# Masks added to the scores by TensorE for half of the batches, and all sixteen early weight tiles decoded in PSUM

## The chip, the cores and the metric

One Trainium2 chip; the kernel uses one of its cores. The metric is device time in microseconds (us) for one execution, and shorter is better. The engines are TensorE (PE in the profile, its weight loads PEld), VectorE (DVE), ScalarE (ACT), GpSimd (POOL) and the queue that issues most transfers (SP). SBUF is the on-chip memory; PSUM, eight banks of 128 partitions by 2 KB, is where TensorE writes.

## The reference

Three stages on 2304 tokens (4 batches of 576):

```python
def _attn_ref(q, k, v):                 # B, H, S, D = 4, 8, 576, 64
    ...
    q_d = q.reshape(B, H, Sd, factor, D).mean(axis=3)     # factor 4, Sd 144
    ...
    out_up = np.repeat(sm_attn(q_d, k_d, v_d), factor, axis=2)
    mask = np.abs(pos[:, None] - pos[None, :]) < factor
    scores = np.where(mask, scale * np.matmul(q, k.transpose(0, 1, 3, 2)), -1000000000.0)
    scores = scores - np.max(scores, axis=-1, keepdims=True)
    attn = np.exp(scores)
    attn = attn / (np.sum(attn, axis=-1, keepdims=True) + 1e-09)
    return out_up + np.matmul(attn, v)
# first feed-forward:  h = x @ w_in;  y = (h * sigmoid(h)) @ w_out     512 -> 2048 -> 512
# second feed-forward: h = x @ w_in2; y = elu(h) @ w_out2              512 -> 2048 -> 512
```

## The kernel before, in words

**Attention.** Sixteen pairs of heads, four per batch, each a call of `attend` (line 563). For one pair: rows of q and k are loaded, transposed by TensorE (line 635) and copied to SBUF; ten windows of 64 by 64 local scores per head go to two PSUM banks, one per head (line 747); VectorE multiplies each bank by a scale, adds the mask and writes the sum to SBUF (`add_mask`, line 758, twice), takes row maxima (line 766, 640 columns for both heads), GpSimd subtracts them (`across`, line 771), ScalarE takes exp (line 777), VectorE sums and inverts (lines 781 to 783), GpSimd multiplies (line 771 again), TensorE transposes (line 853) and multiplies by v (line 920). A pooled branch of 144 by 144 scores runs beside it: sums of q and k on VectorE (line 677), scores (line 800), maxima (line 814), exp (line 822), inverse (lines 832, 833), a scaling on GpSimd (line 839), transposes (line 874), product with pooled v (line 892). Pooled v of batches 1 to 3 comes from two GpSimd additions (lines 709, 710) or from one VectorE reduction (line 714), whichever engine the planner finds free. Both branches are joined into x by VectorE (line 930).

**Weights.** All products of the feed-forward layers are made of three fp32r products of high and low parts, so each weight tile must be split. Before that, the first layer's sixteen tiles of 128 by 1024 words pass a decoder (`decode_jobs`, line 393, called by `prepare`, line 1040): ScalarE takes an absolute value into a temporary (line 411) and converts the low words (line 415), then three steps that need each other: `second`, a clamp (line 419), `third` (line 422) and `fourth` (line 426), both on VectorE. The high part is then copied by ScalarE (line 1054) and the low part subtracted by GpSimd or VectorE (line 1058).

```python
temp = Hold(banks, "w") if i < N_PSUM else None              # prepare, N_PSUM = 8
b = Job("V", 0.70 if inner else 0.45, second, [a], other=None if inner or i >= 2 * FP else ("G", 1.1, lambda: second(nc.gpsimd)))
```

For tiles 0 to 7 the temporary is a PSUM bank (in the rows: `b<-b`), and the clamp is VectorE's; for tiles 8 to 15 it is the SBUF tile `wf`, and the clamp may go to GpSimd.

**Feed-forward during attention.** Six blocks of 256 tokens by eight groups of 256 hidden columns give 48 units (`unit`, line 1068): 12 products into a bank (line 1077), tanh (line 1105), the SiLU product (line 1106) on VectorE, split into high and low (lines 1108, 1111), 12 products into two bank-long accumulators of the block (line 1125). Blocks 0 and 1 run interleaved and need the sixteen tiles one by one. After the last unit, ten passes of 768-column pairs follow (lines 1453, 1541, 1543), which take the rest of the time.

**Who sets the order.** Nothing is ordered by the chip: a planner in the kernel keeps jobs with an engine, a duration, predecessors, PSUM banks they take and use, and due times, and emits them one by one, each to its engine's queue (`pick`, line 293). At any time at most two banks may hold decoder temporaries and at most three unit sums (`bank_rule`, line 344). `LATE` shifts the due times of units of the first two blocks between their two halves. Until unit (0, 0) is emitted, the planner puts products of a zero tile into gaps that it foresees on TensorE (`filler`, line 352); they write to the bank that has been free longest.

Of the kernel before, what the change touches and what calls it, by code (L numbers as in the profile page):

```python
# [22 lines left out]
def attention_moe_moe2_kernel(ctx, tc, q, k, v, wi1, wo1, wi2, wo2, out):  # L23
# [76 lines left out]
    ident = att.tile([P, P], F32, name="ident")  # L100
    mask = att.tile([P, NW // 2, WIN], F32, name="mask")
    xa = xpool.tile([P, KC, 2 * S], F32, tag="xa", name="xa")
# [19 lines left out]
    def constants():  # L122
        make_identity(nc, ident)
        tmp = t_tiles[1][:, :4 * WIN].rearrange("p (n w) -> p n w", w=WIN)
        nc.gpsimd.memset(tmp, 0.0)
        for n, (half, low, high) in enumerate([(0, 0, 6), (0, -3, 3), (1, 0, 6), (1, -3, 3)]):

            for sign, bound in ((1, -low), (-1, high)):
                nc.gpsimd.affine_select(
                    out=tmp[:, n, :], in_=tmp[:, n, :], compare_op=ALU.is_ge, fill=MASKED,  # L130
                    base=bound + sign * WIN * half, pattern=[[sign, WIN]], channel_multiplier=-sign,
                )
        for s in range(NW // 2):
# [218 lines left out]
    def filler(n):  # L352
        if n > 0:
            entry = min(banks.free, key=lambda x: x[:2])
            for _ in range(n):
                nc.tensor.matmul(entry[2], wz[0][:, :P], wz[0][:, :512], start=True, stop=True)

    def fill(t):
        gap = t - clock_of["P"]
        if banks.free:  # L360
            filler(min(int((gap - 0.1) / 0.22), 40))

    wz = []


# [27 lines left out]
    def decode_jobs(i, out, preds, takes=(), temp=None):  # L393
# [169 lines left out]
    def attend(i, due):  # L563
# [171 lines left out]
        for part, (s0, s1, halves_, outs) in enumerate(parts):  # L735
# [18 lines left out]
            psl = follow(Job("P", 0.15 + 0.11 * (s1 - s0) * 2, scores, copies, lat=0.2, takes=held + ([hE] if start_ else []), uses=[hqk], mode="s"), "psl")  # L754
            masked = []
            for j, bank in enumerate(held):
                def add_mask(j=j, bank=bank, s0=s0, s1=s1):
                    nc.vector.scalar_tensor_tensor(
                        E4(s0, s1)[:, :, j, :], bank.tile[:, :(s1 - s0) * WIN].rearrange("p (s w) -> p s w", w=WIN), BSCALE,
                        mask[:, s0:s1], op0=ALU.mult, op1=ALU.add,  # L760
                    )

                masked.append(Job("V", 0.15 + 0.00106 * (s1 - s0) * WIN, add_mask, [psl], uses=[bank]))
            n = 2 * (s1 - s0) * WIN
            top = Job(
                "V", 0.14 + 0.00106 * n, lambda s0=s0, s1=s1: nc.vector.tensor_reduce(col3(hmx, s0, s1), E3(s0, s1), axis=AX.X, op=ALU.max),
                masked, takes=[hmx] if start_ else [], uses=[hmx],
            )
# [4 lines left out]
            less = alike(  # L773
                0.15 + 0.00173 * n, lambda f=across: f(nc.gpsimd, hmx, ALU.subtract),
                0.15 + 0.00106 * n, lambda f=across: f(nc.vector, hmx, ALU.subtract), [top], main="G", uses=[hmx],
            )
            ex = Job("A", 0.21 + 0.00083 * n, lambda s0=s0, s1=s1: nc.scalar.activation(E3(s0, s1), E3(s0, s1), AF.Exp), [less])

# [786 lines left out]
    with tc.manual_schedule():  # L1565
# [138 lines left out]
```

## Time and profile before

| | us |
|---|---|
| median of 3 runs (892.75 to 894.23) | 893.6 |
| the profiled execution, its own time | 893.9 |
| its span (first to last instruction) | 891.5 |
| PE busy in the span | 875.7 (98%) |
| DVE, ACT, POOL busy in the span | 673.1, 540.8, 273.0 |

A row of the profile names line, engine, operation, and the tiles as output <- inputs without their buffer numbers. "Busy" is the union of an engine's instructions; matmuls overlap each other, so a busy PE may still run below its pace. What lies around the span is 2.4 us (893.9 less 891.5).

### The profile page before, as it was taken

Reading aid. Unit: us, or ns where it says so; the run is one execution under the profiler, and the core shown is the slowest. Engines: PE = TensorE matmul, PEld = TensorE weight load, DVE = VectorE, ACT = ScalarE, POOL = GpSimd, SP = SyncE. Lnnn points to the kernel's source line nnn. Section 1 sums busy time; section 2 is a strip of 40 time slices with the busy share of each in tenths; the row PEclk is TensorE's granted clock in tenths of the full one; section 3 lists DMA queues with packets and bytes.
Section 4 is the critical chain, followed back from the end, with each engine's and each line's share of the span. In section 5 each row is a group of like instructions: output and inputs, shape, how many; then the busy total and the mean of one; then the engine's idle time right before and its main releaser. Section 6 shows DMA issues by size and latency. Waiting matters only on the chain.

```text
span 891.5 us, 17228 instructions
## 1 busy us (share of the span) xinstructions
PE 875.7 (98%) x6614; PEld 817.0 (92%) x6614; DVE 673.1 (76%) x1236; ACT 540.8 (61%) x1226; POOL 273.0 (31%) x278
## 2 busy tenths in 40 slices
PE   9989899999999999999999999999999999999998
PEld 6778798999999999999999999898898998998986
DVE  6899768786967988968848969489489888483562
ACT  4796546664547668648347477286497584571650
POOL 4687977875301211401014213001051031010000
PEclk9999899999999999999999999999999999999999
DMA  9896148551134345154432240350520430220301
GB/s 158 217 220 159 54 107 240 119 143 36 69 95 142 106 142 177 48 201 154 130 112 90 83 155 23 107 178 3 186 71 37 165 131 36 90 89 35 107 1 72
DMA packets 105522, 100.08 MB, mean 112 GB/s; under 512 B 62240, under 2 KB 92448, under 8 KB 105312
## 3 DMA queue, kind: packets, MB, share of 16 engines
q1 hardware_dynamic: 103072, 98.39, 37.2%
q8 instruction: 52, 0.85, 0.4%
q10 hardware_dynamic: 2368, 0.59, 0.4%
q14 instruction: 30, 0.25, 0.1%
HBM read 75.37 MB, written 23.59 MB: 111 GB/s over the span
## 4 chain that ended last, share of the span: by engine, by line
PE 90%; DVE 4%; POOL 2%; ACT 1%; DMA 1%; issue 1%; SPq 0%; POOLq 0%; DVEq 0%; ACTq 0%
PE b L1453 33%; PE b L1543 22%; PE b L1541 15%; PE b L1125 6%; PE b L1077 6%; PE b L635 1%; PE b L892 1%; PE b L920 1%; PE b L874 1%; PE b L800 1%; POOL w L1058 1%; PE b L853 1%; PE b L747 1%; DMA nat<-in_q_dram 1%; POOL wf L419 1%
## 5 line engine op out<-in xcount | busy, mean ns | idle before, releaser
L1543 PE MATMUL b<-w,grw 128*128 128x512 f32 x384 | 121.2, 389 | 0.0
L1543 PE MATMUL b<-w,ghk 128*128 128x512 f32 x288 | 99.1, 389 | 0.0
L1453 PE MATMUL b<-xhr,xaw 128*128 128x384 f32 x360 | 96.4, 335 | 0.0
L1541 PE MATMUL b<-grw,w 128*128 128x384 f32 x352 | 91.2, 334 | 0.0
L1543 PEld LDWEIGHTS b<-w,grw 128*128 128x128 f32 x384 | 72.1, 188 | 14.9
L1077 PE MATMUL b<-xh,w 128*128 128x256 f32 x384 | 84.5, 298 | 0.8 <-DVE t L1106 0.8
L1453 PE MATMUL b<-xhr,w 128*128 128x384 f32 x320 | 83.8, 335 | 0.0
L1125 PE MATMUL b<-gh,w 128*128 128x256 f32 x384 | 80.7, 292 | 0.0
L1543 PE MATMUL b<-w,glk 128*128 128x512 f32 x192 | 74.8, 389 | 0.0
L1541 PE MATMUL b<-ghk,w 128*128 128x384 f32 x248 | 71.6, 334 | 0.0
L1077 PEld LDWEIGHTS b<-xh,w 128*128 128x128 f32 x384 | 66.1, 198 | 2.2 <-DVE t L1106 1.2
L1235 POOL TENSOR_TENSOR w<-raw,w 128x512 fp32r<-128x512 f32 x16 | 22.8, 1435 | 144.9 <-ACT w L1233 129.8
L1453 PE MATMUL b<-xlr,xaw 128*128 128x384 f32 x200 | 66.9, 334 | 0.0
L1125 PEld LDWEIGHTS b<-gh,w 128*128 128x128 f32 x384 | 64.1, 193 | 1.5 <-issue 1.2
L1453 PEld LDWEIGHTS b<-xhr,xaw 128*128 128x128 f32 x360 | 65.4, 188 | 0.0
L1543 PEld LDWEIGHTS b<-w,ghk 128*128 128x128 f32 x288 | 54.1, 188 | 11.2
L1541 PEld LDWEIGHTS b<-grw,w 128*128 128x128 f32 x352 | 63.7, 188 | 0.0
L1465 ACT COPY hg<-b 128x384 f32<-128x384 f32 x60 | 28.5, 479 | 50.2 <-PE b L1453 49.2
L1453 PEld LDWEIGHTS b<-xhr,w 128*128 128x128 f32 x320 | 58.0, 188 | 0.2
L1236 DVE TENSOR_TENSOR xlr<-tail,xhr 128x768 fp32r<-128x768 f32 x51 | 49.6, 972 | 11.4 <-ACT xhr L1233 10.8
L1506 DVE SCALAR_TENSOR_TENSOR part<-b,part 128x384 f32<-128x384 f32 (+1 forms) x42 | 25.0, 608 | 43.2 <-PE b L1543 28.4
L1541 PE MATMUL b<-glk,w 128*128 128x384 f32 x168 | 56.1, 334 | 0.0
(262 smaller groups left out, 2443.2 us busy)
## 6 DMA issues: line engine op xcount, KB each, us to landing
ws<-in_moe_w_in_dram SPq DMA_DIRECT2D x32, 512.0 KB
ws<-in_moe_w_out_dram SPq DMA_DIRECT2D x31, 512.0 KB
tail<-x SPq DMA_DIRECT2D x24, 384.0 KB
x<-part SPq DMA_DIRECT2D x6, 768.0 KB
out_dram<-part SPq DMA_DIRECT2D x18, 256.0 KB
vw<-in_v_dram SPq DMA_DIRECT2D x28, 144.0 KB
tail<-xd SPq DMA_DIRECT2D x10, 384.0 KB
natv<-in_v_dram SPq DMA_DIRECT2D x22, 144.0 KB
```

The source lines that it names most:

```text
L419: eng.tensor_scalar(tf, tf, 2.0, W_MAX, op0=ALU.max, op1=ALU.min)
L635: nc.tensor.transpose(bank.tile[:, n * TB:(n + 1) * TB], row(which, c)[:TB], ident[:TB, :TB])
L747: nc.tensor.matmul(held[j].tile[o:o + WIN, c:c + WIN], qT[j * D:(j + 1) * D, q0[w]:q0[w] + WIN], kT[j * D:(j + 1) * D, w0[w]:w0[w] + WIN], ...
L1077: nc.tensor.matmul(ph.tile[:, :NB0], w[a][:, c, :], x_slot(n, c, b_), start=start and m == 0, stop=stop and m == len(products) - 1,)
L1125: nc.tensor.matmul(y[d // 2].tile[:, o:o + NB0], w[m // 2][:, sl], gg(m % 2), start=f == 0 and m == 0 and d % 2 == 0, stop=fin and m == 2, ...
L1235: "G", GPS_[width], lambda: nc.gpsimd.tensor_tensor(lo(), src, hi().bitcast(F32), ALU.subtract), [a], due=due,
L1236: other=("V", VEC_[width], lambda: nc.vector.tensor_tensor(lo(), src, hi().bitcast(F32), ALU.subtract)),
L1453: nc.tensor.matmul(acc_, a[:, cs], b[:, c, :], start=fresh and c == 0 and m == 0, stop=c == 1 and m == 2, skip_group_check=True,)
L1465: snap[after, j] = [Job("A", ACT_[NB], lambda dst=dst, acc_=acc_: nc.scalar.copy(dst, acc_), [], gate, due=soon)]
L1506: nc.vector.scalar_tensor_tensor(dst, src, sc, dst, op0=ALU.mult, op1=ALU.add)
L1541: nc.tensor.matmul(y[d][:, :NB], wm[:, sl], gm, start=first, stop=last_)
L1543: nc.tensor.matmul(y[d], gm[:, sl], wm, start=first, stop=last_)
```

## The change

1. For batches 0 and 1 (`MASK_PE = 2`) TensorE puts the mask into both score banks before the scores: four products per pair of heads, each of a 64 by 64 unit matrix with 320 columns of a bf16 mask; the scores are accumulated on top. VectorE then takes the maxima straight from each bank (two reductions of 128x320) and subtracts them from each bank (two instructions of 128x320); the scale moves into the exp. The GpSimd subtraction of these eight pairs is gone. Four VectorE instructions at the start build the second half of the mask and the unit matrix.
2. All sixteen weight tiles use a PSUM bank as the decoder's temporary (`N_PSUM = 16`), and the clamp is always VectorE's.
3. The products of zeros write to one bank of their own, which is held until unit (0, 0) is emitted.
4. `LATE` is 1.2 instead of 1.0.

```diff
-    QUAD_FROM = 2
+    QUAD_FROM, MASK_PE = 2, 2
...
-    LATE, FRAC = 1.0, (0.25, 0.5, 0.75, 1.0)
-    SLACK, MOST_H, N_PSUM, SPLIT_F = 0.05, 3, 8, 3
+    LATE, FRAC = 1.2, (0.25, 0.5, 0.75, 1.0)
+    SLACK, MOST_H, N_PSUM, SPLIT_F = 0.05, 3, 16, 3
...
+        for p in range(0, P, WIN):
+            nc.vector.tensor_copy(masks[p:p + WIN, 1], mask[WIN - p:P - p])
+            nc.vector.tensor_copy(unit_[p:p + WIN, :], ident[p:p + WIN, p:p + WIN])
...
     def filler(n):
         if n > 0:
-            entry = min(banks.free, key=lambda x: x[:2])
             for _ in range(n):
-                nc.tensor.matmul(entry[2], wz[0][:, :P], wz[0][:, :512], start=True, stop=True)
+                nc.tensor.matmul(fill_bank.tile, wz[0][:, :P], wz[0][:, :512], start=True, stop=True)
...
-        b = Job("V", 0.70 if inner else 0.45, second, [a], other=None if inner or i >= 2 * FP else ("G", 1.1, lambda: second(nc.gpsimd)))
+        b = Job("V", 0.70 if inner else 0.45, second, [a])
...
+                if b < MASK_PE:
+                    for j in range(2):
+                        for o in range(2):
+                            nc.tensor.matmul(
+                                held[j].tile[o * WIN:(o + 1) * WIN, :(s1 - s0) * WIN], unit_[j * WIN:(j + 1) * WIN, :],
+                                masks[j * WIN:(j + 1) * WIN, o ^ j, s0:s1].rearrange("p s w -> p (s w)"),
+                                start=True, stop=False, skip_group_check=True,
+                            )
...
-                            start=True, stop=True,
+                            start=b >= MASK_PE, stop=True, skip_group_check=b < MASK_PE,
...
+            if b < MASK_PE:
+                for j in range(2):
+                    top = Job(
+                        "V", 0.14 + 0.00053 * n, lambda j=j, mx4=mx4, bank3=bank3: nc.vector.tensor_reduce(mx4(j), bank3(j), axis=AX.X, op=ALU.max),
...
+                    def minus(j=j, mx4=mx4, bank3=bank3, s0=s0, s1=s1):
+                        nc.vector.tensor_tensor(E4(s0, s1)[:, :, j, :], bank3(j), mx4(j).to_broadcast([P, s1 - s0, WIN]), ALU.subtract)
...
+                ex = Job("A", 0.21 + 0.00083 * n, lambda s0=s0, s1=s1: nc.scalar.activation(E3(s0, s1), E3(s0, s1), AF.Exp, scale=BSCALE), less)
...
+        fill_bank.take()
         filler(WARM)
...
         run(g1_jobs[FILL_TO])
         filling[0] = False
+        fill_bank.done(g1_jobs[FILL_TO][-1])
```

The planner then orders everything anew. The changed kernel's lines are a little higher: its lines 424, 427 and 431 are the decoder's steps of lines 419, 422 and 426 before, 1092 is 1058, 1140 and 1145 are 1106 and 1111, 714 and 715 are 709 and 710, 719 is 714, 848 is 814, 873 is 839, 1057 is 1023, 964 is 930; `across` stands on line 771 in both.

GpSimd's queue where the last weight tiles are decoded (`wf` is the decoder's SBUF tile, `w` the low part of a weight tile, `ring` the scores in SBUF, `gl` the low part of a unit's activation, `natv` and `vd` the rows of v and their pooled sums). Before:

```order
L1111 TENSOR_TENSOR gl<-t,gh 128x256 [waits PE_49,Activation_49]
L419 TENSOR_SCALAR wf<-wf 128x512 [waits Activation_49]
L771 TENSOR_TENSOR ring_118<-ring_118,small 128x640 [waits DVE_49]
L419 TENSOR_SCALAR wf<-wf 128x512 [waits Activation_49]
L1058 TENSOR_TENSOR w_1526<-wf,w_1526 128x512 [waits Activation_49]
L771 TENSOR_TENSOR ring_118<-ring_118,small 128x640 [waits DVE_49]
L419 TENSOR_SCALAR wf<-wf 128x512 [waits Activation_49]
L839 TENSOR_TENSOR ring_119<-ring_119,small 72x576 [waits DVE_49,Pool_49]
L1058 TENSOR_TENSOR w_1551<-wf,w_1551 128x512
```

and in the changed kernel, where the low parts of the last tiles are made:

```order
L1092 TENSOR_TENSOR w_1545<-wf,w_1545 128x512 [waits Activation_49]
L1092 TENSOR_TENSOR w_1567<-wf,w_1567 128x512 [waits Activation_49]
L714 TENSOR_TENSOR natv<-natv 72x2x128 [waits DMAHW3_49]
L715 TENSOR_TENSOR vd_143<-natv 72x128 [waits PE_49,Pool_49]
L1145 TENSOR_TENSOR gl<-t,gh 128x256 [waits Activation_49]
L1092 TENSOR_TENSOR w_1618<-wf,w_1618 128x512 [waits DMAHW7_49,DMAHW6_49,Activation_49]
L1057 TENSOR_TENSOR xl<-xa,xh 128x256 [waits PE_49,Activation_49] x2
L1145 TENSOR_TENSOR gl<-t,gh 128x256 [waits Activation_49]
L771 TENSOR_TENSOR ring_119<-ring_119,small 128x640 [waits DVE_49]
L873 TENSOR_TENSOR ring_120<-ring_120,small 72x576 [waits DVE_49,Activation_49]
```

The clamps that stood between the two passes over the scores, and ahead of the pooled scaling, are gone, as is the first of the two passes of line 771; additions for pooled v have come in.

VectorE's queue at the last tiles but a few (`b` is a PSUM bank, `ws` the loaded words). Before:

```order
L422 SCALAR_TENSOR_TENSOR wf<-wf,ws 128x512 [waits DMAHW3_49,Pool_49]
L426 SCALAR_TENSOR_TENSOR wf<-ws,wf 128x512 [waits DVE_49]
L422 SCALAR_TENSOR_TENSOR wf<-wf,ws 128x512 [waits DMAHW0_49,Activation_49,Pool_49]
L814 TENSOR_REDUCE small<-b_91 72x2 [waits PE_49]
L814 TENSOR_REDUCE small<-b_98 72x2 [waits PE_49]
L1106 SCALAR_TENSOR_TENSOR t<-t,b_95 128x256 [waits Activation_49]
L426 SCALAR_TENSOR_TENSOR wf<-ws,wf 128x512 [waits DVE_49]
L422 SCALAR_TENSOR_TENSOR wf<-wf,ws 128x512 [waits DMAHW1_49,Activation_49,Pool_49]
```

and in the changed kernel:

```order
L424 TENSOR_SCALAR b_95<-b_95 128x512 [waits Activation_49]
L427 SCALAR_TENSOR_TENSOR b_95<-b_95,ws 128x512 [waits DMAHW4_49,DVE_49]
L431 SCALAR_TENSOR_TENSOR wf<-ws,b_95 128x512 [waits DVE_49,Pool_49]
L424 TENSOR_SCALAR b_92<-b_92 128x512 [waits PE_49,Activation_49]
L427 SCALAR_TENSOR_TENSOR b_92<-b_92,ws 128x512 [waits DMAHW5_49,DVE_49]
L1140 SCALAR_TENSOR_TENSOR t<-t,b_98 128x256 [waits Activation_49]
L431 SCALAR_TENSOR_TENSOR wf<-ws,b_92 128x512 [waits DVE_49,Pool_49]
L424 TENSOR_SCALAR b_95<-b_95 128x512 [waits PE_49,Activation_49]
L427 SCALAR_TENSOR_TENSOR b_95<-b_95,ws 128x512 [waits DMAHW6_49,DVE_49,Activation_49]
```

The third step waited for GpSimd's clamp (Pool in its waits) with a SiLU product queued behind it; now clamp and third step follow each other on VectorE, and the fourth step waits for GpSimd only for the tile that it overwrites.

## Rows read from the trace of the kernel before

**Rows 1.** Stretches: length, busy PE, PEld, DVE, ACT, POOL, granted clock, DMA share, GB/s.

```profile
0.00:46.80 46.80, 44.02 (x714) 32.86 (x714) 35.50 (x82) 28.35 (x91) 25.82 (x44) 1.00 0.91 186
46.80:98.00 51.20, 45.59 (x544) 42.02 (x543) 48.54 (x87) 38.10 (x100) 43.15 (x40) 0.97 0.74 174
98.00:114.50 16.50, 13.06 (x101) 11.10 (x100) 9.25 (x13) 7.54 (x19) 14.10 (x12) 0.69 0.07 26
...
400.00:891.00 491.00, 487.88 (x2545) 453.61 (x2543) 351.27 (x607) 291.43 (x581) 77.59 (x60) 1.00 0.28 93
```

**Rows 2.** The same view for the two stretches at the lower granted clock.

```profile
52.99:56.40 3.41, 3.41 (x28) 2.98 (x28) 3.41 (x8) 3.32 (x11) 3.33 (x5) 0.50 1.20 200
104.19:114.43 10.24, 9.61 (x60) 8.63 (x60) 4.27 (x8) 3.39 (x10) 7.92 (x8) 0.50 0.01 3
```

**Rows 3.** The chain that ended last, pieces of 44 to 125 us: start, length, what.

```profile
90.12 2.34 POOL wf L419
...
99.58 2.02 POOL wf L419
101.62 2.85 DVE wf L422
```

**Rows 4.** Timeline of PE, 98 to 105 us: start, length, what, idle before it and its releaser.

```profile
99.32 0.55 PE L853 MATMUL b<-ident,ring 128*128 128x128 f32 x3 [0.60 <-POOL ring L771]
...
102.75 0.50 PE L874 MATMUL b<-ident,ring 72*72 72x72 f32 x4 [1.16 <-POOL ring L839]
...
104.86 0.58 PE L1077 MATMUL b<-xh,w 128*128 128x256 f32 x1 [0.63 <-DVE t L1106]
```

**Rows 5.** Waits of PE: total us, times, longest.

```profile
PE b L635 <- DMA nat<-in_q_dram: 2.6, 2, 1.9
...
PE b L874 <- DVE wf L426: 1.2, 1, 1.2
PE b L747 <- ACT spare L861: 0.9, 1, 0.9
```

**Rows 6.** Groups of DVE by form, 0 to 140 us: busy us, mean ns of one, idle before.

```profile
L422 DVE SCALAR_TENSOR_TENSOR wf<-wf,ws 128x512 int32<-128x512 int32 x8 | 8.8, 1111 | 2.2 <-POOL wf L419 2.2
L758 DVE SCALAR_TENSOR_TENSOR ring<-b,mask 128x320 f32<-128x320 f32 x18 | 8.0, 479 | 1.7 <-PE b L747 1.7
...
L766 DVE TENSOR_REDUCE small<-ring 128x10 f32<-128x640 f32 x9 | 7.2, 803 | 0.1
...
L426 DVE SCALAR_TENSOR_TENSOR wf<-ws,wf 128x512 int32<-128x512 int32 x8 | 6.8, 851 | 0.0
...
L714 DVE TENSOR_REDUCE vd<-natv 72x128 f32<-72x512 f32 x5 | 5.2, 1065 | 0.0
L422 DVE SCALAR_TENSOR_TENSOR b<-b,ws 128x512 int32<-128x512 int32 x7 | 4.7, 688 | 0.0
L426 DVE SCALAR_TENSOR_TENSOR wf<-ws,b 128x512 int32<-128x512 int32 x7 | 4.7, 671 | 0.0
L419 DVE TENSOR_SCALAR wf<-wf 128x512 f32<-128x512 f32 x2 | 4.3, 2132 | 0.0
```

**Rows 7.** All clamps of line 419: ns least, median, most; first and last start.

```profile
L419 DVE TENSOR_SCALAR raw<-raw x48: 409/421/1114, 260.3 to 730.4; 128x512 f32<-128x512 f32 x48
L419 DVE TENSOR_SCALAR b<-b x8: 687/692/700, 32.0 to 65.0; 128x512 f32<-128x512 f32 x8
L419 POOL TENSOR_SCALAR wf<-wf x6: 1914/2210/2355, 67.7 to 105.3; 128x512 f32<-128x512 f32 x6
```

**Rows 8.** A group of POOL by form, 0 to 140 us.

```profile
L771 POOL TENSOR_TENSOR ring<-ring,small 128x640 f32<-128x640 f32 x16 | 20.5, 1282 | 14.8 <-DVE small L766 7.7 <-DVE small L783 4.4 <-DVE small L832 1.9
```

**Rows 9.** Timeline of PE, 0 to 20 us, two pieces: start, length, what.

```profile
9.10 1.03 PE L356 MATMUL b<-t 128*128 128x512 bf16 x4
...
14.00 0.81 PE L747 MATMUL b<-tail 64*64 64x64 f32 x40
```

**Rows 10.** All products of zeros: ns least, median, most; first and last start.

```profile
L356 PE MATMUL b<-t x38: 376/379/634, 1.4 to 46.2; 128*128 128x512 bf16 x38
```

More of the change, by code (lines that the diff above doesn't have):

```diff
@@ L100, in attention_moe_moe2_kernel @@
     ident = att.tile([P, P], F32, name="ident")
-    mask = att.tile([P, NW // 2, WIN], F32, name="mask")
+    masks = att.tile([P, 2, NW // 2, WIN], BF16, name="mask")
+    mask = masks[:, 0]
+    unit_ = att.tile([P, WIN], BF16, name="unit")
     xa = xpool.tile([P, KC, 2 * S], F32, tag="xa", name="xa")
@@ L353, in filler @@
         if n > 0:
-            entry = min(banks.free, key=lambda x: x[:2])
             for _ in range(n):
-                nc.tensor.matmul(entry[2], wz[0][:, :P], wz[0][:, :512], start=True, stop=True)
+                nc.tensor.matmul(fill_bank.tile, wz[0][:, :P], wz[0][:, :512], start=True, stop=True)
     def fill(t):
         gap = t - clock_of["P"]
-        if banks.free:
-            filler(min(int((gap - 0.1) / 0.22), 40))
+        filler(min(int((gap - 0.1) / 0.22), 40))
     wz = []
+    fill_bank = Hold(banks, "f")
+    fill_bank.left = 1
     wsrc = [(wi1, wo1), (wi2, wo2)]
@@ L415, in half, with second @@
             nc.scalar.activation(st[:, :, 0].bitcast(U32), st[:, :, 0].bitcast(U32), AF.Copy, scale=2.0 ** -29, bias=2.0 ** -10 - 0.5)
-        def second(eng=nc.vector):
+        def second():
             tf = t().bitcast(F32)
-            eng.tensor_scalar(tf, tf, 2.0, W_MAX, op0=ALU.max, op1=ALU.min)
+            nc.vector.tensor_scalar(tf, tf, 2.0, W_MAX, op0=ALU.max, op1=ALU.min)
         def third():
@@ L750, in scores @@
                             kT[j * D:(j + 1) * D, w0[w]:w0[w] + WIN],
-                            start=True, stop=True,
+                            start=b >= MASK_PE, stop=True, skip_group_check=b < MASK_PE,
                         )
[L754 to L763, printed above, removed]
+            psl = follow(Job("P", (0.4 if b < MASK_PE else 0.15) + 0.11 * (s1 - s0) * 2, scores, copies, lat=0.2, takes=held + ([hE] if start_ else []), uses=[hqk], mode="s"), "psl")
@@ L764, in attend @@
             n = 2 * (s1 - s0) * WIN
[L765 to L768, printed above, removed]
             def across(eng, h, op, s0=s0, s1=s1):
                 eng.tensor_tensor(E3(s0, s1), E3(s0, s1), col3(h, s0, s1).to_broadcast([P, 2 * (s1 - s0), WIN]), op)
[L773 to L776, printed above, removed]
@@ L777, in attend, with add_mask @@
-            ex = Job("A", 0.21 + 0.00083 * n, lambda s0=s0, s1=s1: nc.scalar.activation(E3(s0, s1), E3(s0, s1), AF.Exp), [less])
+            if b < MASK_PE:
+                mx4 = lambda j, s0=s0, s1=s1: hmx.tile.rearrange("p (s j o) -> p s j o", j=2, o=1)[:, s0:s1, j, :]
+                bank3 = lambda j, held=held, s0=s0, s1=s1: held[j].tile[:, :(s1 - s0) * WIN].rearrange("p (s w) -> p s w", w=WIN)
+                less = []
+                for j in range(2):
+                    top = Job(
+                        "V", 0.14 + 0.00053 * n, lambda j=j, mx4=mx4, bank3=bank3: nc.vector.tensor_reduce(mx4(j), bank3(j), axis=AX.X, op=ALU.max),
+                        [psl], takes=[hmx] if start_ and j == 0 else [], uses=[hmx],
+                    )
+                    def minus(j=j, mx4=mx4, bank3=bank3, s0=s0, s1=s1):
+                        nc.vector.tensor_tensor(E4(s0, s1)[:, :, j, :], bank3(j), mx4(j).to_broadcast([P, s1 - s0, WIN]), ALU.subtract)
+                    if j:
+                        top.after([first_top])
+                    first_top = top
+                    less.append(Job("V", 0.15 + 0.00053 * n, minus, [top], uses=[hmx, held[j]]))
+                ex = Job("A", 0.21 + 0.00083 * n, lambda s0=s0, s1=s1: nc.scalar.activation(E3(s0, s1), E3(s0, s1), AF.Exp, scale=BSCALE), less)
+            else:
+                masked = []
+                for j, bank in enumerate(held):
+                    def add_mask(j=j, bank=bank, s0=s0, s1=s1):
+                        nc.vector.scalar_tensor_tensor(
+                            E4(s0, s1)[:, :, j, :], bank.tile[:, :(s1 - s0) * WIN].rearrange("p (s w) -> p s w", w=WIN), BSCALE,
+                            mask[:, s0:s1], op0=ALU.mult, op1=ALU.add,
+                        )
+                    masked.append(Job("V", 0.15 + 0.00106 * (s1 - s0) * WIN, add_mask, [psl], uses=[bank]))
+                top = Job(
+                    "V", 0.14 + 0.00106 * n, lambda s0=s0, s1=s1: nc.vector.tensor_reduce(col3(hmx, s0, s1), E3(s0, s1), axis=AX.X, op=ALU.max),
+                    masked, takes=[hmx] if start_ else [], uses=[hmx],
+                )
+                less = alike(
+                    0.15 + 0.00173 * n, lambda f=across: f(nc.gpsimd, hmx, ALU.subtract),
+                    0.15 + 0.00106 * n, lambda f=across: f(nc.vector, hmx, ALU.subtract), [top], main="G", uses=[hmx],
+                )
+                ex = Job("A", 0.21 + 0.00083 * n, lambda s0=s0, s1=s1: nc.scalar.activation(E3(s0, s1), E3(s0, s1), AF.Exp), [less])
```

## The prediction

> **What bounds the kernel now.** I read the stretches first. From 400 us on TensorE (PE) is busy 487.88 of 491 us at full clock [rows 1]; that part is paced by its own products, the change touches nothing in it, and what the change can move lies in the attention stage before. There the three stretches to compare are the start up to 46.8 us, the stretch to 98 us in which the first two feed-forward blocks run as their weight tiles are decoded, and the short one to 114.5 us. In the second, PE idles 51.20 - 45.59 = 5.6 us while VectorE is busy 48.54 of 51.20: VectorE is what PE follows. In the third PE idles 16.50 - 13.06 = 3.4 us, VectorE is busy only 9.25 of 16.5, but GpSimd 14.10: the wait has gone over to GpSimd [rows 1].
>
> Then the granted clock. Two stretches, 3.41 and 10.24 us long, ran at 0.50, the lower of PE's two levels [rows 2]; work done there takes twice its time, so they cost half their length, 1.7 and 5.1 us. The second begins at 104.19 us, right behind a row of waits of PE [rows 4].
>
> Then the chain that ended last. Between 90 and 104 us it does not run along PE, but along clamps on GpSimd (2.34 and 2.02 us on the chain) and a third decoder step on VectorE that took 2.85 us [rows 3]. The third step takes 0.688 us when its temporary is in PSUM, 1.111 on average when it is in SBUF [rows 6]: on the SBUF form VectorE loses time while GpSimd works. The pot, then, is 5.6 + 3.4 us of idle time and 1.7 + 5.1 us of clock, 15.8 us in all.
>
> **Decoding in PSUM.** Eight tiles change form. On VectorE: eight third steps 8 x (1.111 - 0.688) = 3.4 us less; eight fourth steps 8 x (0.851 - 0.671) = 1.4 us less; clamps, 8 x 0.692 = 5.5 us instead of the 4.3 us of the two that VectorE had, 1.3 us more [rows 6, 7]. Together 3.5 us less. GpSimd loses six clamps of 2.21 us, 13.3 us [rows 7]. As the order shows, these stood ahead of passes over the scores and of the pooled scaling, for which PE waited.
>
> **What the planner then moves.** Ahead of the seventeenth SiLU product VectorE's queue holds two reductions of pooled v where it held six; GpSimd takes the others as additions. 4 x 1.065 = 4.3 us less on VectorE [rows 6].
>
> **The mask.** GpSimd loses one pass over 640 columns for each of eight pairs, 8 x 1.282 = 10.3 us [rows 8]. VectorE had 2 x 0.479 + 0.803 = 1.76 us per pair; now two reductions and two subtractions of 320 columns out of PSUM, for which the nearest row is the mask addition itself (320 columns out of PSUM, 0.479), so 1.92 us: 0.16 more, 0.6 us for the four pairs of batch 1 [rows 6]. PE gets four products of 320 columns per pair. A product of 512 columns takes (1.03 - 0.38) / 3 = 0.217 us when issued back to back (four in 1.03 us, one by itself 0.379); 320 columns are then 0.136 us, 0.54 us per pair if one follows the other. But 40 products of 64 columns took 0.81 us, 0.020 each against 0.027 at that pace, so products on parts of the array overlap somewhat: three quarters, 0.41 us per pair [rows 9, 10]. For batch 1 that is 1.6 to 2.2 us; I take 1.9, in the middle, since the new ones are long like the first kind and small like the second. Batch 0's four pairs lie in the start, where PE fills gaps with 38 products of zeros (8.2 us at 0.217) [rows 10]: I cost them at nothing; without that cover they'd be another 2 us.
>
> Here a rule bears on the price. The Trainium skill, TensorEngine Tiling (Array Packing), Key Properties, says that the quarters of the array work independently of each other. By it the four mask products of a pair, each on its own quarter, would run at once, 0.14 us per pair and 0.5 us instead of 1.9. The rows show only a partial overlap, so I stay with 1.9; by the rule the sum below would give 883.8.
>
> **The bank for the products of zeros; the due times; the queues.** The fillers no longer wait for a bank's last reader, a small matter, and take one of eight banks from the rest until unit (0, 0). `LATE` issues nothing; it only reorders. On SP the v windows of the first pair now go ahead of the q rows of the third, and a weight tile goes ahead of batch 1's first rows. VectorE's four extra copies at the start fall into its 46.8 - 35.5 = 11.3 us of idle time [rows 1]. I take zero for all of this, covered by the fillers, and allow 1 us either way.
>
> **The sum.** VectorE sheds 3.5 + 4.3 - 0.6 = 7.2 us in a stretch where PE idles 5.6. It cannot give back the wait for a q transfer (1.9) and that for ScalarE's copy (0.9) [rows 5]; 2.8 us are left, which 7.2 us cover. Between 98 and 105 us, the waits for a pass over scores (0.60), the pooled scaling (1.16) and a SiLU product stuck behind the slow third step (0.63) go, 2.4 us [rows 4]; the turns between PE and ScalarE there stay. Without those waits PE does not fall idle before 104 us, and I take the second low stretch as gone, 5.1 us; the first, behind a transfer, stays. 2.8 + 2.4 + 5.1 - 1.9 = 8.4 us. The profiled execution took 893.9 us, so 885.5; the median of the runs is 0.3 lower, so **885.2**.
>
> A second rule speaks against the change. The Trainium skill, VectorE: DVE Perf Modes, "Why PSUM operands drop a tier", says that a VectorE operation with an operand in PSUM loses the faster mode that SBUF gives. The rows agree where GpSimd is quiet: the clamp takes 0.421 us in SBUF and 0.692 in PSUM. But in the stretch at issue VectorE's SBUF clamps took 2.13 us and GpSimd's 2.21 [rows 6, 7]. By that rule alone the eight tiles would cost VectorE 8 x 0.27 = 2.2 us more instead of 3.5 less; it would shed only 1.5 us, and the sum would be 7.1 us, 886.5.
>
> **Rivals.** *The clock falls again.* PE, still tied to a VectorE queue that is nearly full, idles somewhere else and loses its clock for as long. For it: two falls in one execution. Against it: from 400 us on, where work for PE is always ready, there is none [rows 1]. Price 5.1 us: 890.3.
>
> *Banks run short, and it is slower.* PE already waited 1.2 us to write pooled transposes until a fourth decoder step was done [rows 5], that is for a bank which the decoder had. Now eight more tiles hold a bank each, while blocks 0 and 1 hold four of eight for accumulators, and two score banks are held for 1.92 us instead of 0.96. If each of the eight costs PE such a wait, that is 9.6 us, and with PE idle the clock falls again: 2.8 + 2.4 - 1.9 = 3.3 us gained, 9.6 lost, 899.9. It decides from three such waits on (3.3 / 1.2). Against it: the tiles are done sooner, and the planner counts banks.
>
> *It wasn't what PE waited for.* The transfers were (DMA share 0.91 and 0.74 [rows 1]), and faster decoding only waits for words. Then the idle time and both falls stay and the mask is paid: 893.6 + 1.9 = 895.5. Against it: from 98 us on the share is 0.07, and the chain names clamps.
>
> **How the numbers follow.** Forecast 0.58, clock 0.20, banks 0.12, transfers 0.10. Low end: the whole pot of 15.8 us recovered, with the mask at 1.6, gives 879.4; high end: the clock rival with half of the waits left as well (2.6 us), 892.9. Banks and most of the transfers case lie outside, some 0.2. A measurement of this kernel tells 0.2%, 1.8 us, from no change. Faster by more: nearly all of the forecast (0.56) and three quarters of the clock rival (0.15), 0.71. Slower: banks (0.11) and half of the transfers case (0.05), 0.16. The rest, 0.13, is within.
>
> **What would show it.** Right: no clamp on GpSimd; the third step at about 0.69 us for all sixteen; the last tile decoded before 101 us, where the chain of now still has a third step; no stretch at clock 0.50 behind 100 us; PE idle between 46.8 and 115 us below 4 us. Wrong: waits of PE for decoder steps, or for subtractions out of score banks, of 1 us each; a long stretch at 0.50; mask products that take over 0.6 us per pair; a first unit later than now.

## The result, and the profile after

The changed kernel takes 884.17 us, the median of 4 runs (883.56 to 885.28), beside 893.37 us of the kernel before on the same chip (892.75 to 894.23, 4 runs): a ratio of 0.9898 (95% interval 0.9881 to 0.9915), 9.2 us faster. The prediction said 885.2 and 8.4 us less. The profiled execution was the slowest of the four, 885.28 us with a span of 883.2; two of the others ran at a mean granted clock of 1.000.

The same stretches in the changed kernel (columns as in [rows 1], which they answer; the last one as [rows 2]):

```profile
0.00:46.80 46.80, 43.44 (x700) 31.82 (x701) 36.08 (x88) 27.86 (x88) 21.73 (x42) 1.00 0.92 192
46.80:98.00 51.20, 47.73 (x585) 44.23 (x587) 44.13 (x89) 40.82 (x102) 38.47 (x43) 0.97 0.72 169
98.00:114.50 16.50, 16.35 (x229) 15.16 (x220) 10.73 (x27) 10.49 (x32) 11.16 (x15) 1.00 0.39 99
400.00:883.00 483.00, 479.59 (x2497) 445.35 (x2495) 343.97 (x594) 284.25 (x567) 76.52 (x59) 1.00 0.28 93
59.46:62.87 3.41, 3.41 (x18) 2.81 (x19) 2.05 (x5) 2.50 (x6) 3.10 (x4) 0.50 1.25 229
```

PE's idle time between 46.8 and 98 us is 3.5 us (5.6 before), and between 98 and 114.5 us 0.15 us (3.4 before). One stretch at clock 0.50 is left, of 3.41 us; the long one behind 104 us is gone. VectorE is busy 44.1 us of the 51.2, where it was 48.5.

The longest waits of PE up to 140 us (total, times, longest), which answer [rows 5]:

```profile
PE b L640 <- DMA nat<-in_q_dram: 1.5, 1, 1.5
PE b L360 <- DVE t L1601: 1.4, 1, 1.4
PE b L1111 <- DVE wf L431: 1.3, 1, 1.3
PE b L640 <- ACT tail L668: 1.2, 1, 1.2
PE b L887 <- POOL ring L771: 0.9, 1, 0.9
```

Only one wait, 1.3 us, is for a decoder step. Groups of VectorE from 0 to 140 us, which answer [rows 6] and [rows 7]; the clamps of `b` on line 424 are now the only ones of that stage, and there is none on GpSimd:

```profile
L424 DVE TENSOR_SCALAR b<-b 128x512 f32<-128x512 f32 x16 | 11.1, 693 | 2.3 <-ACT b L416 2.0
L427 DVE SCALAR_TENSOR_TENSOR b<-b,ws 128x512 int32<-128x512 int32 x15 | 10.4, 693 | 1.1 <-ACT ws L420 0.8
L431 DVE SCALAR_TENSOR_TENSOR wf<-ws,b 128x512 int32<-128x512 int32 x15 | 10.2, 678 | 0.3
L780 DVE TENSOR_REDUCE small<-b 128x5 f32<-128x320 f32 x16 | 7.5, 480 | 1.0 <-PE b L760 0.8
L785 DVE TENSOR_TENSOR ring<-b,small 128x320 f32<-128x320 f32 x14 | 6.1, 478 | 0.0
L719 DVE TENSOR_REDUCE vd<-natv 72x128 f32<-72x512 f32 x2 | 2.1, 1074 | 0.0
```

All three steps take 0.68 to 0.69 us on average; the last fourth step starts at 98.3 us. On PE's timeline, a set of four mask products is followed 0.16 us later by the scores, the kind of products that [rows 9] showed alone (start, length, what):

```profile
12.32 0.33 PE L752 MATMUL b<-mask,unit 64*64 64x320 bf16 x4
12.48 0.75 PE L760 MATMUL b<-tail 64*64 64x64 f32 x40
```

The chain that ended last, from 94 to 99 us, where [rows 3] had clamps on GpSimd:

```profile
94.33 1.63 PE b L1159 x12
95.96 1.45 PE b L1111 x12
...
97.91 0.43 DVE t L1140
...
98.39 3.13 PE b L1111 x24
```

It runs along PE but for the tanh (0.39 us, among the lines left out) and the SiLU product of one unit, during which PE does mask products and scores of a pair.

**Where the time came from.** Take as lost, for PE, the time between the starts of two products beyond the usual distance of such a product at full clock (0.120 us for a unit's 256 columns, for instance), with a product of zeros lost as a whole. It adds up, in the two profiled executions, so:

| us lost by PE | 0 to 46.8 | 46.8 to 98 | 98 to 114.5 | later | sum |
|---|---|---|---|---|---|
| before | 16.4 | 11.0 | 9.6 | 8.3 | 45.3 |
| changed | 18.2 | 8.7 | 1.4 | 7.5 | 35.8 |

That is 9.5 us less; 32 mask products at 0.037 us (a set of four takes 0.14 to 0.16) are 1.2 us more work; 8.3 us remain, the difference of the spans (891.5 and 883.2).

### The profile page after: what moved, and what is told of

It reads as the page before. It is cut to its first block, busy times and chain, and to the rows that moved or that the text cites. A ratio compares the mean times of both kernels' runs of the same rounds, so it can differ in the third digit from the quotient of the medians.

```text
span 883.2 us, 17347 instructions
## 1 busy us (share of the span) xinstructions
PE 872.6 (99%) x6656; PEld 815.0 (92%) x6656; DVE 662.0 (75%) x1248; ACT 542.4 (61%) x1228; POOL 253.3 (29%) x272
## 4 chain that ended last, share of the span: by engine, by line
PE 95%; SPq 1%; DMA 1%; POOL 1%; DVE 0%; issue 0%; ACT 0%; ACTq 0%; POOLq 0%; DVEq 0%
PE b L1487 33%; PE b L1577 22%; PE b L1575 15%; PE b L1159 8%; PE b L1111 8%; PE b L640 1%; PE b L954 1%; PE b L926 1%; PE b L908 1%; PE b L887 1%; PE b L834 1%; PE b L760 1%; DMA rows<-in_k_dram 1%; PE b L992 1%; SPq L607 1%; SPq L593 0%
## 5 line engine op out<-in xcount | busy, mean ns | idle before, releaser
L1111 PE MATMUL b<-xh,w 128*128 128x256 f32 x384 | 81.8, 292 | 1.5 <-DVE wf L431 1.3
L1111 PEld LDWEIGHTS b<-xh,w 128*128 128x128 f32 x384 | 64.3, 193 | 3.6 <-ACT xh L1053 1.4
```

The source lines that it names most:

```text
L1111: nc.tensor.matmul(ph.tile[:, :NB0], w[a][:, c, :], x_slot(n, c, b_), start=start and m == 0, stop=stop and m == len(products) - 1,)
```

## Experiments

Each was timed with the kernel before on the same chip, whose medians there were 893.2 to 894.0 us. Differences of single kernels below about 2 us are not told apart. All but runs 7 to 10 also make the planner order everything anew.

**1. Sixteen tiles alone**, in the kernel before:

```diff
-    SLACK, MOST_H, N_PSUM, SPLIT_F = 0.05, 3, 8, 3
+    SLACK, MOST_H, N_PSUM, SPLIT_F = 0.05, 3, 16, 3
-        b = Job("V", ..., second, [a], other=None if inner or i >= 2 * FP else ("G", 1.1, lambda: second(nc.gpsimd)))
+        b = Job("V", 0.70 if inner else 0.45, second, [a])
```

> Only the sixteen tiles in PSUM, mask, fillers and due times as before. If the end of the decoding is what cost (GpSimd clamps, the slow third step, the fall of the clock behind them): most of the gain, 885 to 888 us, and no stretch at clock 0.50 behind 100 us. If the mask's move is what pays: 892 to 894 us. If it is only the new order as a whole: anywhere, and the low stretch need not go.

886.94 us (884.29 to 888.03), ratio 0.9926 (0.9907 to 0.9946). Its stretches:

```profile
46.80:98.00 51.20, 47.15 (x549) 43.39 (x548) 45.30 (x91) 41.76 (x105) 43.61 (x49) 0.93 0.84 194
98.00:114.50 16.50, 16.50 (x214) 15.88 (x213) 9.36 (x22) 9.37 (x32) 11.93 (x14) 1.00 0.16 40
50.63:57.45 6.82, 6.08 (x44) 5.30 (x48) 6.46 (x13) 6.13 (x16) 6.74 (x9) 0.50 1.17 256
```

(The profiled execution was the fastest of its four.) Without the mask part PE is never idle from 98 to 114.5 us and the long stretch at 0.50 is gone: this one number gives 893.2 - 886.9 = 6.3 us.

**2. The mask part alone**, in the kernel before: all edits of the change that stand under `MASK_PE`, eight tiles with clamps on GpSimd, no own bank, `LATE` 1.0.

```diff
-    QUAD_FROM = 2
+    QUAD_FROM, MASK_PE = 2, 2
...
```

> Only the mask on TensorE and the subtraction out of PSUM; eight tiles still decoded in SBUF with clamps on GpSimd. If the end of the decoding is what cost: 890 to 894 us, a third step of over 1 us on average and a stretch at 0.50 still there. If the GpSimd passes of 1.28 us over the scores were the cost: 885 to 888 us.

895.54 us (895.16 to 903.96, 10 runs), ratio 1.0032 (1.0011 to 1.0054): slower. The profiled execution was the odd one at 903.96 us, so only its steps are read here, not its sums. Its chain still runs along clamps behind which low parts stand:

```profile
97.24 0.88 POOL wf L424
98.11 0.70 POOL gl L1145
98.81 2.51 POOL w L1092 x2
...
101.80 2.36 POOL wf L424
```

Freeing GpSimd of eight passes over the scores does not take the clamps off the path.

**3. The changed kernel with eight tiles**, and the choice of GpSimd for the clamp back.

```diff
-    SLACK, MOST_H, N_PSUM, SPLIT_F = 0.05, 3, 16, 3
+    SLACK, MOST_H, N_PSUM, SPLIT_F = 0.05, 3, 8, 3
-        b = Job("V", 0.70 if inner else 0.45, second, [a])
+        b = Job("V", ..., second, [a], other=None if inner or i >= 2 * FP else ("G", 1.1, lambda: second(nc.gpsimd)))
```

> The changed kernel with eight instead of sixteen tiles decoded in PSUM, and the choice of a GpSimd clamp back for the others. If the sixteen decoded tiles are what pays (running them alone in the kernel before gave back 6.3 of 9.2 us): the waits at 98 to 105 us and the long low-clock stretch behind 100 us return, 891 to 896 us, near the run of the mask part alone (895.2 to 895.7 us). The rival, that the mask products and the changed order shorten the path by themselves once the late-bound of 1.2 is in: 885 to 888 us with PE's idle time in 98 to 114.5 us below 1 us.

892.89 us (891.21 to 897.18), ratio 0.9996 (0.9979 to 1.0013): the whole gain is gone. Six clamps are on GpSimd again, and the third steps of those tiles are slow again (groups from 0 to 140 us, then the stretch):

```profile
L424 POOL TENSOR_SCALAR wf<-wf 128x512 f32<-128x512 f32 x6 | 13.0, 2175 | 1.5 <-ACT wf L416 1.3
L427 DVE SCALAR_TENSOR_TENSOR wf<-wf,ws 128x512 int32<-128x512 int32 x8 | 9.4, 1190 | 0.8 <-POOL wf L424 0.8
```

```profile
98.00:114.50 16.50, 12.64 (x126) 11.48 (x125) 12.23 (x17) 8.59 (x21) 13.94 (x12) 0.90 0.39 97
```

PE idles 3.9 us there. The stretch at 0.50 is only 3.41 us long this time (the mean clock is 0.90, not 0.69).

**4. The changed kernel without mask products.**

```diff
-    QUAD_FROM, MASK_PE = 2, 2
+    QUAD_FROM, MASK_PE = 2, 0
```

> The changed kernel without mask products (masks of batches 0 and 1 are added on VectorE and subtracted on GpSimd as before); sixteen tiles in PSUM, own bank and late-bound stay. Theory: the mask part is small once the decoded tiles are early: 885.5 to 888 us, that is 1.5 to 4 us slower than the change, with no stretch of low clock behind 100 us. Rival: the mask is needed to keep VectorE in time, then idle time of more than 1 us at 98 to 114.5 us, a second low-clock stretch, and 889 us or more. Second rival: the mask gains nothing and costs TensorE time, 884 us or less.

886.97 us (886.36 to 888.31), ratio 0.9920 (0.9899 to 0.9941), the first theory. Waits of PE from 46.8 to 140 us, the two longest:

```profile
PE b L1111 <- POOL xl L1057: 1.7, 1, 1.7
PE b L1111 <- ACT ring L856: 1.0, 1, 1.0
```

GpSimd, which keeps its eight passes, makes a low part of x 1.7 us too late. On top of the sixteen tiles the mask part is worth 887.0 - 884.2 = 2.8 us by the medians, 2.0 by the ratios, whose intervals overlap; alone it cost 2 to 3. Beside run 1, with the same tiles and no mask products (886.94), the own bank and `LATE` together make no difference that can be told.

**5. Only the clamp moved**: the kernel before, every clamp on VectorE, eight temporaries still in SBUF.

```diff
-        b = Job("V", ..., second, [a], other=None if inner or i >= 2 * FP else ("G", 1.1, lambda: second(nc.gpsimd)))
+        b = Job("V", 0.70 if inner else 0.45, second, [a])
```

> Kernel before with one edit: the clamp of the eight SBUF tiles is VectorE's alone, so GpSimd has none, but the temporary stays in SBUF. If GpSimd's clamps in front of its passes were the cost: 886 to 889 us. If the SBUF form itself is (VectorE's steps held up while GpSimd works): 890 to 894 us, with clamps of about 2 us and third steps over 1 us on VectorE.

889.25 us (887.79 to 890.91), ratio 0.9948 (0.9928 to 0.9969): 4 of the 6.3 us of run 1. The three steps on SBUF (groups 0 to 140 us):

```profile
L419 DVE TENSOR_SCALAR wf<-wf 128x512 f32<-128x512 f32 x8 | 10.5, 1325 | 0.0
L426 DVE SCALAR_TENSOR_TENSOR wf<-ws,wf 128x512 int32<-128x512 int32 x8 | 7.0, 869 | 0.0
L422 DVE SCALAR_TENSOR_TENSOR wf<-wf,ws 128x512 int32<-128x512 int32 x8 | 6.5, 820 | 0.2
```

They take 1.325 + 0.820 + 0.869 = 3.0 us a tile, against 0.693 + 0.693 + 0.678 = 2.06 in PSUM. The clamps on SBUF (ns least, median, most), the stretch from 98 us, and the times of one short clamp and of the longest (columns as in [rows 1]):

```profile
L419 DVE TENSOR_SCALAR wf<-wf x8: 414/923/4050, 72.2 to 106.6; 128x512 f32<-128x512 f32 x8
98.00:114.50 16.50, 13.15 (x161) 11.88 (x161) 14.07 (x20) 9.78 (x27) 12.21 (x12) 0.90 0.39 102
85.17:85.59 0.42, 0.42 (x6) 0.42 (x5) 0.42 (x3) 0.42 (x1) 0.00 (x0) 1.00 0.80 154
99.98:104.03 4.05, 3.07 (x30) 2.46 (x29) 4.03 (x2) 3.78 (x10) 3.74 (x4) 1.00 0.65 145
```

Four of the eight clamps took 0.41 to 0.42 us, three of them with GpSimd idle throughout; the other four took 1.4 to 4.05 us, each with GpSimd at work for most of it. For the eight tiles VectorE spends 24.0 us here, more than the 8.8 + 6.8 + 4.3 = 19.9 of before [rows 6], and the kernel is 4 us faster all the same. What the edit relieves is GpSimd's queue; how much of the 4 us is that, and how much the new order, the run doesn't part. PE's idle time from 98 to 114.5 us did not go with the clamps: 16.50 - 13.15 = 3.4 us, as before. Only the low clock behind it is shorter (granted clock 0.90, 0.69 before). It is with the steps in PSUM (run 1) that PE is busy throughout that stretch; the 2.3 us between the two medians are hardly more than the measurement tells.

**6. Twelve tiles in PSUM**, all else as in the changed kernel.

```diff
-    SLACK, MOST_H, N_PSUM, SPLIT_F = 0.05, 3, 16, 3
+    SLACK, MOST_H, N_PSUM, SPLIT_F = 0.05, 3, 12, 3
```

> The changed kernel with twelve tiles decoded in PSUM instead of sixteen; the clamps of the last four, on VectorE too, go on SBUF. If what counts is that no step on VectorE runs on SBUF beside GpSimd, four such tiles (twelve steps, each 0.3 to 1.5 us longer than 0.69 us by the groups of the kernel before) put some of the waits back: 886 to 890 us. If what counts is only that no clamp goes to GpSimd: within 1 us of the change, 883.5 to 885.2 us, or below it as fewer banks are taken.

884.94 us (884.03 to 887.30), ratio 0.9912 (0.9892 to 0.9932): as fast as sixteen. The last four tiles' steps on SBUF:

```profile
L431 DVE SCALAR_TENSOR_TENSOR wf<-ws,wf 128x512 int32<-128x512 int32 x4 | 4.4, 1103 | 0.0
L427 DVE SCALAR_TENSOR_TENSOR wf<-wf,ws 128x512 int32<-128x512 int32 x4 | 2.7, 688 | 0.0
L424 DVE TENSOR_SCALAR wf<-wf 128x512 f32<-128x512 f32 x4 | 2.1, 520 | 1.1 <-ACT wf L416 1.1
```

2.3 us a tile: only the fourth step is slow here, four tiles lose 4 x (2.31 - 2.06) = 1 us in all, and I had expected 3.6 us or more. The sixteen are not needed as sixteen.

**7. PE kept busy through the waits, a miss.** Products of constants in the kernel before, ahead of the transposes of the pair with index 7:

```diff
+    KEEP = 7
...
+                    if i == KEEP and g0 == 0:
+                        for _ in range(6):
+                            nc.tensor.matmul(bank.tile[:, :2 * P], ident.bitcast(BF16)[:, :P], ident.bitcast(BF16), start=True, stop=True)
...
```

> Kernel before with 16 products of constants (256 columns, about 0.11 us each) put ahead of the transposes of the last pair of batch 1, into banks that these overwrite; the order is the same otherwise, and the waits for GpSimd stay. If idling ahead of 104 us makes the clock fall and the fall costs half its length: no long stretch at 0.50 and 888 to 889 us. If the clock would fall anyway, or its fall costs little: 893 to 894 us.

896.06 us (893.39 to 897.12), ratio 1.0025 (1.0013 to 1.0037). The trace shows that the products went elsewhere, behind the stretch in question:

```profile
L855 PE MATMUL b<-ident x6: 272/273/282, 126.6 to 127.2; 128*128 128x256 bf16 x6
```

So the run does not say what makes the clock fall. It does show that the long fall is no accident of one execution: from 98 to 114.5 us the granted clock is 0.69 here too. And where PE does not wait, such products cost about what they take: 16 at 0.11 us are 1.8, the ratio says 2.2 (1.2 to 3.3).

**8. The same at the right pair**, with products ahead of all four groups of transposes.

```diff
+    KEEP = 6
...
+                    if i == KEEP:
+                        for _ in range(5 if g0 else 6):
...
+                    if i == KEEP:
+                        for _ in range(5 if a else 10):
...
```

> The kernel before with 26 products of constants (256 columns, about 0.11 us each) put ahead of the transposes of the pair at 98 to 105 us, 6 and 5 ahead of the two groups of L853's transposes, 10 and 5 ahead of the two of L874's: TensorE works through the waits for GpSimd and ScalarE that stay. Theory, that the clock falls at 104 us because of this idle time: the 10.24 us stretch at 0.50 goes or is much shortened, PE idle at 98 to 104 us drops by 2 us or more, and the time falls by 3 to 5 us, to 888 to 890 us. Rival, that the clock falls for another reason (or later, all the same): the stretch stays, at most shifted, and the time is 893 to 896 us.

890.92 us (888.62 to 891.49, 8 runs), ratio 0.9961 (0.9944 to 0.9977), 3.5 us by the ratio. Stretches:

```profile
51.29:58.11 6.82, 6.13 (x44) 5.34 (x48) 6.34 (x12) 6.31 (x17) 6.74 (x9) 0.50 1.10 269
98.00:114.50 16.50, 15.35 (x193) 13.67 (x192) 12.50 (x21) 9.59 (x26) 15.29 (x14) 1.00 0.21 53
104.20:114.43 10.23, 9.75 (x133) 8.84 (x131) 7.57 (x13) 5.16 (x15) 9.04 (x10) 1.00 0.15 33
```

Clamps and decoder steps are left as before; only PE works where it stood (busy 5.43 us from 98 to 104.1, 3.29 before), and the stretch that ran at 0.50 [rows 2] runs at 1.00. So it was what PE did, and did not do, from 98 to 104 us that brought the clock down: with work in its idle time it does not fall. Most of PE's work there was transposes, and whether other work with the same gaps would have kept the clock was not tried. Nor does the sum of the idle time alone set the length of a fall: from 98 to 114.5 us PE idles 3.9 us in run 3 and 3.4 in run 5, with 3.41 us at 0.50, and 3.4 us in the kernel before, with 10.24. In the profiled execution of this run the earlier stretch at 0.50 was 6.82 us instead of 3.41, which takes 1.7 of the 5.1 us back.

**9. The same in the changed kernel**, 12 products ahead of the transposes at 57.9 us and 8 ahead of those at 59.5 us.

```diff
+                if i == 6 and n_ == 0:
+                    for _ in range(12):
...
+                    if i == 4 and g0 == 0:
+                        for _ in range(8):
...
```

> The changed kernel with 20 products of constants (256 columns) in the waits at 56.6 to 59.4 us: 12 ahead of the transposes at 57.89 us, 8 ahead of those at 59.45 us. The only low-clock stretch left starts at 59.46 us, right behind these waits, and costs 3.41 x 0.5 = 1.7 us. If it falls because of the idle time: no stretch near 60 us, 882 to 883.5 us. If the first wait is for the bank itself, the 12 products come behind it and cost 1.3 us instead: 884.5 to 886 us, with the stretch shifted or still there.

884.44 us (884.10 to 885.00), ratio 0.9904 (0.9885 to 0.9923): no difference that can be told from the change. PE's timeline there (idle time before, with its releaser, in brackets):

```profile
57.23 1.47 PE L635 MATMUL b<-ident 128*128 128x256 bf16 x12 [1.17 <-ACT tail L671]
58.54 0.58 PE L643 MATMUL b<-ident,spare 96*128 96x96 f32 x5
58.96 1.04 PE L891 MATMUL b<-ident 128*128 128x256 bf16 x8
```

The stretch at 0.50 near 60 us is gone in this execution. But the first wait is for the bank itself, so the 12 products stand behind it and cost 58.54 - 57.23 = 1.3 us. And two of the changed kernel's own four executions ran at a mean clock of 1.000 without them, with spans of 881.5 and 881.9 us; here three at 1.000 took 882.0 to 883.0.

**10. The mask products ten times over**, for batch 1's four pairs, 36 sets more:

```diff
+                    for _ in range(10 if b == 1 else 1):
```

> The changed kernel with the four mask products of each of batch 1's four pairs issued ten times over (the last set is kept, so the sums are the same): 36 sets more. If the four run side by side, 0.16 us a set as the profile of the change has it for one set: 36 x 0.16 = 5.8 us, so about 890 us. If they run one behind the other, at the 0.40 to 0.55 us a set of the prediction: 14 to 20 us, so 898 to 904 us. Batch 0's sets are left alone.

888.73 us (887.76 to 890.95), 4.6 us above the change; ratio to before 0.9947 (0.9925 to 0.9969). One of the four places on PE's timeline:

```profile
49.88 1.55 PE L753 MATMUL b<-mask,unit 64*64 64x320 bf16 x40
51.26 0.75 PE L761 MATMUL b<-qk 64*64 64x64 f32 x40
```

Ten sets in 51.26 - 49.88 = 1.38 us, 0.138 each; 36 of them are 5.0 us. One product of 320 columns is 0.136 us at the pace of the products of zeros (an estimate, 320/512 of 0.217), so four on four quarters take no longer than one.

**11. Products of zeros without their own bank**, all else as changed.

```diff
+            entry = min(banks.free, key=lambda x: x[:2])
...
-                nc.tensor.matmul(fill_bank.tile, wz[0][:, :P], wz[0][:, :512], start=True, stop=True)
+                nc.tensor.matmul(entry[2], wz[0][:, :P], wz[0][:, :512], start=True, stop=True)
...
```

> The changed kernel with the products of zeros written to whichever bank is free, as before, and so one bank more for the work up to the first unit. In the run without mask products the bank and the late-bound together were worth nothing (886.97 us beside 886.94 us of sixteen tiles alone). Theory: the own bank is worth nothing here either, 883 to 886 us. Rival, that the bank taken away is what costs about 2 us of TensorE at 30 to 40 us: 881.5 to 883 us with the first unit before 40 us. Rival on the other side, that fillers without their own bank fail where all banks are taken: 886.5 us or more, with fewer fillers and a longer low-clock stretch.

887.89 us (887.63 to 890.26), ratio 0.9946 (0.9929 to 0.9963): 3.7 us slower than the change, the rival on the other side, though not by its low clock (five of its six executions ran at 0.999 or 1.000). The products of zeros up to 47 us, here and in the change:

```profile
L361 PE MATMUL b<-t 128*128 128x512 bf16 x48 | 15.3, 445 | 4.6 <-DVE t L1601 1.4 <-ACT ring L856 1.2 <-ACT yo L856 1.2
L360 PE MATMUL b<-t 128*128 128x512 bf16 x48 | 14.2, 422 | 1.4 <-DVE t L1601 1.4
```

The 48 products themselves wait 3.2 us for last readers of the bank they were given (ScalarE's copies), with real work queued behind them; the first unit starts at 46.92 us, in the change at 40.81. In the order without mask products the bank and `LATE` together made no difference that can be told (run 4 beside run 1).

**12. `LATE` at 1.4.**

```diff
-    LATE, FRAC = 1.2, (0.25, 0.5, 0.75, 1.0)
+    LATE, FRAC = 1.4, (0.25, 0.5, 0.75, 1.0)
```

> The changed kernel with the late-bound at 1.4 instead of 1.2. No trace here shows what it is worth; in the run without mask products it and the bank were worth nothing. Theory: it only moves a few steps of TensorE's order, 882.5 to 886 us. Rival: the order matters by more than that, outside these bounds on either side.

890.83 us (888.48 to 892.33, 12 runs), ratio 0.9966 (0.9951 to 0.9980): the rival; 6.7 us of the gain are lost by order alone. Waits of PE from 47 to 140 us:

```profile
PE b L1111 <- DVE small L866: 2.1, 1, 2.1
PE b L887 <- POOL ring L771: 1.2, 1, 1.2
```

Neither stands in the list of the change with such length. Why the planner's order comes out so differently I did not follow. Since the order alone moves the time by 6.7 us, no single run above that changes it shows by its time alone what a part is worth. Taken together the runs do show that the clamps on GpSimd cost time: by the medians no kernel without them took more than this run's 890.8 us, and of those with them none took less than 892.9 but run 8 (890.9), where PE works through the waits.

No version here beats the change by more than a measurement tells.

## Why the prediction was right, point by point

- **Decoding in PSUM.** The sum of the steps was right: sixteen tiles now take 16 x (0.693 + 0.693 + 0.678) = 33.0 us of VectorE, 36.4 by [rows 6, 7] before; 3.4 us less, forecast 3.5. Run 3 shows that without it nothing is gained, run 1 that it alone gives most. Run 5 adds that some 4 of run 1's 6.3 us come when only the clamps leave GpSimd, though VectorE then spends more time on the tiles, not less.
- **Idle time from 46.8 to 98 us**: 2.8 forecast; 5.6 - 3.5 = 2.1 by busy time, 2.3 by the table of lost time. That the number is near is in part luck. VectorE was to shed 7.2 us; its busy time there fell by 48.5 - 44.1 = 4.4. Of the four reductions of pooled v that were to leave (4.3 us), three lie in this stretch. And the two waits that were to stay, for a q transfer (1.9) and for a copy by ScalarE (0.9), are not there any more: the 3.5 us left are one wait for a decoder step (1.3), one for another copy (1.2) and one for a pass over scores (0.9).
- **Waits and clock behind 98 us**: 2.4 + 5.1 = 7.5 forecast, 8.2 by the table. The step "Without those waits PE does not fall idle before 104 us" held, the second low stretch went with it, and run 8 shows by itself that work in that idle time keeps the clock up. The turns between PE and ScalarE, which were to stay, went as well: PE idles 0.15 us there. That the waits went because GpSimd has no clamps is not shown: in run 5 it has none and PE idles as before. The rival that the clock falls again elsewhere did not come. A stretch of 3.41 us at 0.50 stayed in the profiled execution, as forecast, but at 59.46 us instead of 52.99, behind waits for ScalarE (1.2) and GpSimd (0.9) and not behind a transfer; and not in all: two of the four ran at 1.000.
- **The mask on PE was mis-sized.** 1.9 us for batch 1, in the middle between no overlap (2.2) and the part of an overlap that I read from the rows (1.6); four sets at 0.16 us are 0.64. The rule that I weighed against the rows and did not follow, the Trainium skill, TensorEngine Tiling (Array Packing), Key Properties (quarters work independently), was right: 0.138 us a set in run 10, against the 0.14 worked out by it. What misled me was my reading of [rows 9], not the rows. I divided the whole 0.81 us by 40, though one such product lasts 0.218 us by itself (first row below, the middle number) and I had taken a lone product out of the 1.03 us beside it; done alike it is (0.81 - 0.22) / 39 = 0.015 us from start to start, not 0.020. And the pace of 0.027 us was that of bf16 products, while these are f32 (20 products of the kernel, each of which the trace has twice). The trace shows the first four starting within 0.02 us of each other (second row, of a timeline that ends at 14.03 us), and, further on, the next four each time 0.058 us later: four side by side were there to be read.

```profile
L747 PE MATMUL b<-tail x160: 217/218/367, 11.7 to 88.0; 64*64 64x64 f32 x160
14.00 0.29 PE L747 MATMUL b<-tail 64*64 64x64 f32 x4
```

- **Zero for the start was too kind**: PE lost 18.2 - 16.4 = 1.8 us more there, and batch 0's mask products, costed at nothing, are in the 1.2 us of the table below. These misses cancel nearly, and that the two sums differ by 0.1 us only is luck:

| us gained | forecast | by the table of lost time |
|---|---|---|
| 0 to 46.8 us | 0 | -1.8 |
| idle time, 46.8 to 98 us | 2.8 | 2.3 |
| waits and clock, 98 to 114.5 us | 2.4 + 5.1 | 8.2 |
| later | 0 | 0.8 |
| mask products | -1.9 | -1.2 |
| sum | 8.4 | 8.3 |

- **The bank was not "a small matter"**: run 11 puts it, with the order that comes of it, at 3.7 us. The first unit came 3.4 us earlier than before.
- **PSUM against SBUF on VectorE.** The Trainium skill, VectorE: DVE Perf Modes, "Why PSUM operands drop a tier", says that with an operand in PSUM VectorE loses the faster mode that SBUF gives; by that alone the prediction made the eight tiles 2.2 us dearer for VectorE. The trace agrees for the clamp while GpSimd is idle (0.42 us on SBUF, 0.69 on PSUM), not for this stage: 3.0 us a tile on SBUF in run 5, 2.06 on PSUM. The Trainium skill, SBUF — State Buffer, "Who interferes with whom", says that a VectorE instruction with two inputs in SBUF contends with a GpSimd instruction that reads SBUF, and that one in a mode that takes both ports and one of GpSimd block each other for a whole instruction. The stretched steps of [rows 6, 7] and the clamps of run 5, short with GpSimd idle and long beside its work, agree with it; no run here parts it from another cause.
- **Rivals.** Banks: one wait for a decoder step of 1.3 us, the same as the 1.2 before [rows 5], where three were needed to decide. Transfers: the wait for q of 1.9 us at 51.56 us is gone; the 1.5 us of now stand at 9.28 us, in the start, where it was 0.7. The share of the DMA from 46.8 to 98 us is as before (0.72, 0.74), and the idle time and the time fell; by this rival both would have stayed.

What stays open: the parts do not add up (the mask part costs 2 to 3 us alone and gives 2 to 3 on top, which is near what can be told; the bank gives nothing that can be told, with `LATE`, or 3.7). Each makes the planner order everything anew, and how much of a difference is the part and how much the order was not measured. `LATE` 1.0 within the changed kernel was not run.

## What to carry to other kernels

When the chain leaves the busiest engine for a second, slower one (here clamps on GpSimd), ask what a step costs beside that engine's work, not alone: PSUM was slower for a lone clamp and faster for the stage. Count a stretch of low clock as part of the price of the idle time ahead of it; filling the gap with useless products shows how much. Before trusting a part's worth, run it alone and also take it out of the whole: for the mask part the two answers differed in sign. And where a planner orders everything anew, look how much the order alone can move (6.7 us here).

## What the runs showed of the hardware that I had not expected

- Four products on four quarters of the array take as long as one: 0.138 us for a set of 320 columns, beside 0.136 for one, worked out from the products of zeros.
- One and the same kernel is granted different clocks from run to run: the change 0.997 to 1.000, with spans of 883.2 and 881.5 us at the ends; the profiled execution of the change had one stretch at 0.50, and in those at 1.000 there can be none of that length.
- A clamp of 512 columns on SBUF took VectorE 0.41 to 0.42 us with GpSimd idle and up to 4.05 us beside its work (run 5); on PSUM it never took more than 0.70 us, in any run.
